# Two PSUM banks that hold K over each change of layer, and an earlier place for the filling unit's denominators and heads, in a two-layer decode kernel

## The chip, the cores and the metric

The kernel runs on one core of a Trainium2 chip. The metric is the device time of one execution in microseconds (us). Before the change the median of three runs is 2507.16 us (2505.84 to 2508.34). The profile comes from one more execution, which took 2507.28 us; its instructions span 2505.5 us.

## What is computed

Two identical rounds are run over a state `x` of 2 batches x 512 values. A round is an attention block over a cache (32 query heads in 8 groups, so 8 K and V heads of 128 values, 32768 cached positions), and then a mixer, a small MLP over each value of the normalised row:

```python
x = x + attention(layernorm(x), k_cache, v_cache, wq, wo)
x = x + mixer(layernorm(x), w1, b1, w2, b2)      # w2 @ gelu(w1 * ln(x) + b1) + b2, 1792 hidden
x = x + attention(layernorm(x), k_cache, v_cache, wq, wo)   # the same caches and weights again
x = x + mixer(layernorm(x), w1, b1, w2, b2)
```

Everything is fp32. K and V of both batches together are 536.9 MB, and both rounds read all of them, so most of the kernel is a stream of cache data from HBM.

## The kernel before

**Units, granules, steps.** A unit is (layer, batch, K/V head). It has 64 granules of K and 64 of V. A granule is 128 partitions x 512 fp32 (256 KB), and it takes one *cell* of the SBUF tile `mem`, which has 106 cells. A step consumes 4 granules: `k_step` (L333) is four score matmuls at L340 into a `scores` bank, `v_step` (L384) four matmuls at L393 into the bank `acc`. A granule's matmul shows as 2 rows of the profile, so a step is 8 rows. Between K and V of a unit lie the maximum (L354, L362), the transposes (L370) and the exponentials (L375).

**Order.** `Order` (L43) writes out the list of 1024 steps. While V of one unit runs, the K of the next has been read. At a change of layer the attention of one batch ends, its mixer runs, and the next layer's first K of that batch can only start when the mixer has given its query. `changes` (L67) names, for each of the two batches, three units: `x`, the last unit of layer 0 for the batch; `fill`, a unit of the other batch whose V is streamed while the mixer runs; and `y`, the first unit of layer 1, which has the same cache head as `x`. Since `x` and `y` read the same K and V, some of it is kept in `mem` and loaded once: `KEPT_K` = 10 granules of K and all 64 of V (L85 to L90). Those 74 cells are taken through the change, and what streams has to go through the other 32.

**Work around a change.** `at(p, f, ...)` hangs a function behind step `p` (L712). With `e` the last V step of `x` (the fill's V begins at `e` + 1): the head sums `out_1` and the output product `out_2` of `x`, the first mixer normalisation (`mix_1`, `mix_2`), seven pairs of gelu tiles with their `project` (L510) behind steps `e` + 3 to `e` + 10, `take_rows` (L468) which copies the bank `rows`, and `change_0` to `change_3` (L570 to L599) behind `e` + 11 to `e` + 14, which make the query of `y`. `unread` (L604) are matmuls whose result nobody reads; they keep TensorE busy. The filling unit's own `denominators` (L412) stand at its fifth V step, its `out_1` 7 steps and its `out_2` 9 steps behind its last V step, that is, among the K steps of `y` (L766, L781 to L783).

**PSUM.** Eight banks: two for `scores`, `acc`, `rows0` and `rows1` (one for each batch), `bcast` for the mixer's input, and two that the pool `misc` turns through for all small results and for the query products.

**Loads.** All loads are issued from one queue (SP, L833 for K and V, L828 for weights), in the order in which the steps need them, each with a count of granules, a first cell, and the step behind which it is issued. `plan_loads` (L117) chooses cells and step beforehand with its own estimates: it takes the largest piece and the highest cells that it thinks cost no wait (`reversed(spots)`, L164). The sizes around a change are laid down by `cut` (L92 to L99): the fill's V and the K of `y` come four granules at a time, except the first load of K of `y`, which has `-KEPT_K % STEP` = 2 granules. At run time the load waits until the instructions that used its cells are done.

**The end.** The last unit's V is loaded in pieces of 16, 16, 16, 8, 4, 2, 1 and 1 granules; `last_mixer` (L627) then does the last head sums, mixer and output.

Of the kernel before, what the change touches and what calls it, by code (L numbers as in the profile page):

```python
# [10 lines left out]
ALU = mybir.AluOpType  # L11
# [11 lines left out]
KEPT_V = 64  # L23
SIZES = (32, 24, 16, 8, 4)
# [18 lines left out]
class Order:  # L43


    def __init__(self, heads):
# [70 lines left out]
def plan_loads(order, weights, busy):  # L117
# [7 lines left out]
    from_kept = set(order.kept.values())  # L125
# [16 lines left out]
    while i < len(asked) or weights:  # L142
# [58 lines left out]
def gqa_mixer_kernel(ctx: ExitStack, tc: tile.TileContext, x, kt, v, wqo, cols, out):  # L201
# [6 lines left out]
    FT = (cols.shape[1] - 1) // 3  # L208
# [11 lines left out]
    pmisc = ctx.enter_context(tc.tile_pool(name="pmisc", bufs=2, space=bass.MemoryType.PSUM))  # L220
# [9 lines left out]
    cols_sb = const.tile([P, 3 * FT + 1], F32, name="cols_sb")  # L230
    w1c, b1c, w2c = (cols_sb[:, k * FT : (k + 1) * FT] for k in range(3))
    b2c = cols_sb[:, 3 * FT : 3 * FT + 1]
# [6 lines left out]
    sel1 = selg[:, 0:1].to_broadcast([P, P])  # L239
    qz = const.tile([P, 28 + 32 * SLOTS], F32, name="qz")  # L240
    acc = pfix.tile([P, G], F32, name="acc")
    rows = [pfix.tile([P, G], F32, name=f"rows{b}") for b in range(B)]
# [3 lines left out]
    xT = {}  # L246

    def constants():
# [9 lines left out]
        nc.vector.memset(acc, 0.0)  # L258
        for t in rows:
            nc.vector.memset(t, 0.0)  # L260

    def first_input():
# [4 lines left out]
        p = pmisc.tile([P, G], F32, name="misc")  # L267
# [6 lines left out]
        p = pmisc.tile([P, G], F32, name="misc")  # L274
# [12 lines left out]
    q_at, q_ps, q_row, turn = {}, {}, {}, [0]  # L287
# [13 lines left out]
    def wide_products(us, wq):  # L301

        q_ps[us] = pmisc.tile([P, G], F32, name="misc")
# [3 lines left out]
    def narrow_products(us, side):  # L307

        n = side.shape[1]
        pt = pmisc.tile([P, G], F32, name="misc")  # L310
# [43 lines left out]
    def max_1(u):  # L354
        mxa = work.tile([P, 1], F32, name="mxa")
        nc.vector.tensor_reduce(mxa, mx[u], axis=AX.X, op=ALU.max)  # L356
        pm = pmisc.tile([P, G], F32, name="misc")
# [4 lines left out]
    def max_2(u):  # L362
        pm = pmisc.tile([P, G], F32, name="misc")
# [3 lines left out]
        lsum[u] = work.tile([P, 2, R], F32, name="lsum")  # L367

# [43 lines left out]
    def denominators(u):  # L412
        pl = pmisc.tile([P, G], F32, name="misc")
# [12 lines left out]
    thin = rows[0]  # L426
    po_of = {}

    def out_sum(u):
        po_of[u] = pmisc.tile([P, G], F32, name="misc")  # L430
# [9 lines left out]
    def out_1(u):  # L440
# [5 lines left out]
        oT[u] = work.tile([P, R], F32, name="oT")  # L446
        nc.vector.tensor_mul(oT[u], po[:, :R], rl[u])  # L447
# [5 lines left out]
    def out_2(u):  # L453
        layer, b, h = u
        for r in range(R):
            nc.tensor.matmul(  # L456
                rows[b][32 * r : 32 * r + 1, :],
                oT[u][:, r : r + 1],
# [441 lines left out]
```

## Time and profile before

| | before |
|---|---|
| median of three runs | 2507.16 us |
| the profiled execution | 2507.28 us |
| its span, first to last instruction | 2505.5 us |
| TensorE busy | 1394.1 us |
| VectorE busy | 180.5 us |
| ScalarE busy | 185.8 us |
| read from HBM | 1064.33 MB |
| mean rate over the span | 425 GB/s |

PE stands for TensorE matmuls, PEld for its weight loads, DVE for VectorE, ACT for ScalarE, POOL for GpSimd, SP for the engine whose queue issues the loads. In a timeline row the columns are start, duration, engine, line, operation, output and inputs, and in brackets the idle time of the engine just before with what ended it. A chain or wait that ends in "DMA mem<-in_kt_dram" ended when a load of K landed.

### The profile page before, as it was taken

How to read it: one execution, taken by the hardware profiler on the slowest of the kernel's cores; microseconds unless marked ns; L12 is line 12 of the kernel's file. 1: busy time of each engine (PE TensorE's matmuls, PEld its weight loads, DVE VectorE, ACT ScalarE, POOL GpSimd, SP SyncE). 2: the span in 40 equal slices, each digit the busy share in tenths (PEclk: the TensorE clock that was granted, in tenths of full speed). 3: DMA queues.
4: the chain of work that ended last, by engine and by line, in shares of the span. 5: the costliest groups of instructions: out<-in, count | busy, mean ns of one | idle time of the engine just before them, and what ended most of it. 6: DMA issues, size and time to landing. Idle time of an engine off the chain costs nothing. (4 is left out here: it accounts for less than half of the span.)

```text
span 2505.5 us, 21221 instructions
## 1 busy us (share of the span) xinstructions
PE 1394.1 (56%) x9682; PEld 398.7 (16%) x9682; DVE 180.5 (7%) x487; ACT 185.8 (7%) x579; POOL 5.2 (0%) x18
## 2 busy tenths in 40 slices
PE   3455455554555545556676674555555545564567
PEld 1111111111111111112121121111111111111112
DVE  1000000000000000001010010000000000000012
ACT  0100000000000000001110100000000000000021
POOL 0000000000000000000000000000000000000000
PEclk8777777777777777778888887677777777777788
DMA  9999999999999999999999999999999999999996
GB/s 419 435 432 433 433 432 431 434 429 437 435 431 433 433 430 430 428 429 411 404 426 424 401 430 434 433 434 431 432 435 428 433 434 432 433 434 431 434 428 268
DMA packets 35523, 1065.70 MB, mean 425 GB/s; under 512 B 4197, under 2 KB 4201, under 8 KB 5354
## 3 DMA queue, kind: packets, MB, share of 16 engines
q1 hardware_dynamic: 35144, 1064.32, 98.9%
q8 instruction: 76, 1.25, 0.2%
q14 instruction: 13, 0.11, 0.0%
q10 hardware_dynamic: 290, 0.03, 0.0%
HBM read 1064.33 MB, written 0.00 MB: 425 GB/s over the span
## 5 line engine op out<-in xcount | busy, mean ns | idle before, releaser
L393 PE MATMUL acc<-mem,S 128*16 128x512 f32 x4080 | 595.8, 719 | 600.0 <-DMA mem<-in_v_dram 595.2
L340 PE MATMUL scores<-mem,qz 128*32 128x512 f32 x4096 | 607.0, 735 | 484.4 <-DMA mem<-in_kt_dram 484.2
L375 ACT ACTIVATE S<-S,neg 128x128 f32<-128x128 f32 x256 | 129.6, 509 | 2243.0 <-DVE S L370 1208.4
L340 PEld LDWEIGHTS scores<-mem,qz 128*32 128x32 f32 x4096 | 136.4, 129 | 885.1 <-issue 466.0
L393 PEld LDWEIGHTS acc<-mem,S 128*16 128x16 f32 x4080 | 125.0, 107 | 922.8 <-issue 830.8
L350 DVE TENSOR_REDUCE mx<-scores 128x1 f32<-128x512 f32 x64 | 44.3, 692 | 758.5 <-PE scores L340 750.7
L432 PEld LDWEIGHTS misc<-selg,row 128*128 128x128 f32 x256 | 50.5, 294 | 49.7 <-issue 40.1
L432 PE MATMUL misc<-selg,row 128*128 128x4 f32 x256 | 53.3, 331 | 3.3 <-DVE row L424 3.3
L370 DVE STREAM_TRANSPOSE S<-scores 128x512 f32<-128x512 f32 x64 | 45.5, 711 | 125.4 <-PE acc L393 125.4
L456 PE MATMUL rows<-mem,oT 128*1 128x512 f32 x248 | 51.2, 915 | 0.3 <-DVE oT L447 0.3
L375 ACT ACTIVATION_READ_ACCUMULATOR S<-S,neg 128x1 f32 x256 | 47.7, 186 | 0.0
L360 DVE TENSOR_REDUCE m<-misc 1x4 f32<-1x128 f32 x32 | 8.9, 279 | 381.2 <-PE misc L358 381.2
L424 DVE COPY row<-acc 128x512 f32<-128x512 f32 x32 | 22.1, 692 | 181.6 <-PE acc L393 181.6
L418 DVE RECIPROCAL rl<-misc 128x4 f32<-128x4 f32 x32 | 5.9, 183 | 369.9 <-PE misc L416 369.9
L447 DVE TENSOR_TENSOR oT<-misc,rl 128x4 f32<-128x4 f32 x32 | 5.2, 163 | 293.1 <-PE misc L432 292.6
L416 PEld LDWEIGHTS misc<-both,one 128*128 128x128 f32 x64 | 14.4, 281 | 50.6 <-issue 46.0
L305 PE MATMUL misc<-mem,xw 128*32 128x512 f32 x144 | 19.6, 618 | 1.9 <-DVE xw L281 1.9
L312 PEld LDWEIGHTS misc<-selg,row 128*128 128x128 f32 x128 | 17.1, 208 | 19.1 <-issue 10.3
L312 PE MATMUL misc<-selg,row 128*128 128x2 f32 (+1 forms) x128 | 18.5, 266 | 0.8 <-DVE row L297 0.8
L532 ACT ACTIVATE row<-bcast,bias,scale 128x512 f32<-128x512 f32 x21 | 16.3, 778 | 30.5 <-PE rows L516 15.4
L416 PE MATMUL misc<-both,one 128*128 128x4 f32 x64 | 17.2, 340 | 2.0 <-DVE both L415 2.0
L358 PE MATMUL misc<-ident,mxa 128*1 128x128 f32 x64 | 16.1, 344 | 2.1 <-DVE mxa L356 2.1
(119 smaller groups left out, 247.8 us busy)
## 6 DMA issues: line engine op xcount, KB each, us to landing
mem<-in_v_dram SPq DMA_DIRECT2D x13, 4096.0 KB, 26.6
mem<-in_v_dram SPq DMA_DIRECT2D x37, 1024.0 KB, 8.8
mem<-in_kt_dram SPq DMA_DIRECT2D x16, 2048.0 KB, 17.0
mem<-in_kt_dram SPq DMA_DIRECT2D x30, 1024.0 KB, 7.6
mem<-in_wqo_dram SPq DMA_DIRECT2D x28, 1024.0 KB, 36.4
mem<-in_kt_dram SPq DMA_DIRECT2D x7, 4096.0 KB, 30.9
mem<-in_v_dram SPq DMA_DIRECT2D x4, 2048.0 KB, 27.0
mem<-in_kt_dram SPq DMA_DIRECT2D x1, 6144.0 KB
```

The costliest lines, as they stand in the source:

```text
L305: nc.tensor.matmul(q_ps[us][32 * d : 32 * d + 32, :], xw[:, d, :], wq[:, d, :], start=True, stop=True)
L312: nc.tensor.matmul(pt[:, r * n : (r + 1) * n], q_row[us][:, r * DH : (r + 1) * DH], side, start=True, stop=True,)
L340: nc.tensor.matmul(sc_ps[u, half][32 * row : 32 * row + 32, :], qz[:, at : at + 32], cells(at_cell["K", u, g], 1), start=(i == 0), stop=(i ...
L350: nc.vector.tensor_reduce(mx[u][:, half : half + 1], sc_ps[u, half], axis=AX.X, op=ALU.max)
L370: nc.vector.transpose(S[half], sc_ps[u, half])
L375: nc.scalar.activation(s[:, :, h], s[:, :, h], AF.Exp, bias=neg[u][:, h : h + 1], scale=SCALE, accum_out=lsum[u][:, half, h : h + 1],)
L393: nc.tensor.matmul(acc[32 * row : 32 * row + R * QT, :], S[half][:, col : col + R * QT], vc, start=(g < NG), stop=(g >= quads - NG),)
L416: nc.tensor.matmul(pl[:, :R], ones, both, start=True, stop=True)
L424: nc.vector.tensor_copy(asb[u], acc)
L432: nc.tensor.matmul(po_of[u][:, :R], asb[u][:, t * DH : (t + 1) * DH], selg[:, t * R : (t + 1) * R], start=(t == 0), stop=(t == QT - 1 and ...
L456: nc.tensor.matmul(rows[b][32 * r : 32 * r + 1, :], oT[u][:, r : r + 1], wo_of(u)[:, r, :], start=(u == order.first_of[layer, b]), stop=(u ...
L532: nc.scalar.activation(hid[key, f], px[key], AF.Gelu_apprx_tanh, bias=shift[key][:, f : f + 1], scale=slope[key][:, f : f + 1],)
```

## The change

Each kept K now has two more granules, without two more cells. Behind the third K step of `x` the new `hold` copies its granules 10 and 11 from `mem` into two PSUM banks, `held0` and `held1`. Behind the first K step of `y`, when granules 0 and 1 of the kept K have been used, `give_back` copies the banks into those two cells (one copy on ScalarE, one on VectorE), where the third K step of `y` reads them. `y` no longer loads granules 10 and 11; its K is loaded from granule 12 on, in 13 loads of four.

The banks are found by joining others. `rows0` and `rows1` become one bank `rows`, in which each batch has a partition of every group of 32: the weights that were one column become two, one of them zero (`oz`, `w2z`), every product adds onto the bank (`start=False`), and `take_rows` clears its own batch's rows with a multiplication by `keep` behind its copy. The two `misc` banks become one tile with four quarters, of which `quarter()` gives the next; the query products go to `bcast`. `unread` becomes several matmuls of 128 columns. The granules of the last unit that went to `rows0` (`thin`) go to `held0`.

The filling unit's `denominators` go behind the second step of the second half of its V, its `out_1` one step and its `out_2` two steps behind its V, as for other units. Since `plan_loads` decides cells by its estimates, all cells behind the first change come out differently, the end's too.

The core of the diff:

```diff
+HELD = 2
...
+        self.held = {("K", x, KEPT_K + j): ("K", y, KEPT_K + j) for x, _, y in self.changes for j in range(HELD)}
+        self.back = {("K", y, j): ("K", y, KEPT_K + j) for _, _, y in self.changes for j in range(HELD)}
...
-            self.cut("K", y, KEPT_K, (-KEPT_K % STEP,) + (STEP,) * ((2 * HALF - KEPT_K) // STEP))
+            self.cut("K", y, KEPT_K + HELD, (STEP,) * ((2 * HALF - KEPT_K - HELD) // STEP))
...
-                        last_use[a + j] = step_of[k]
+                        last_use[a + j] = step_of[order.back.get(k, k)]
+                if key in order.held:
+                    landed[order.held[key]] = queue + LAND_US
...
-    rows = [pfix.tile([P, G], F32, name=f"rows{b}") for b in range(B)]
+    rows = pfix.tile([P, G], F32, name="rows")
+    held = [pfix.tile([P, G], F32, name=f"held{j}") for j in range(HELD)]
+    misc = pfix.tile([P, G], F32, name="misc")
...
+    def quarter():
+
+        turn[2] += 1
+        k = turn[2] % 4
+        return misc[:, k * P : (k + 1) * P]
...
+    def hold(x):
+
+        for j in range(HELD):
+            nc.vector.tensor_copy(held[j], cells(at_cell["K", x, KEPT_K + j], 1))
+
+    def give_back(y):
+
+        for j in range(HELD):
+            at_cell["K", y, KEPT_K + j] = at_cell["K", y, j]
+            to = cells(at_cell["K", y, j], 1)
+            if j % 2:
+                nc.vector.tensor_copy(to, held[j])
+            else:
+                nc.scalar.activation(to, held[j], AF.Copy)
...
-                rows[b][32 * r : 32 * r + 1, :],
-                oT[u][:, r : r + 1],
+                rows[32 * r : 32 * r + B, :],
+                oT[u][:, 2 * r + 1 - b : 2 * r + 3 - b],
...
-        nc.vector.tensor_copy(ysb[key], rows[key[1]])
+        nc.vector.tensor_copy(ysb[key], rows)
+        nc.vector.tensor_scalar_mul(rows, rows, keep[:, b : b + 1])
...
-        for _ in range(count):
-            nc.tensor.matmul(idle[0][:1, :n], one, S[0][:, :n] if u == order.last else ident[:, :1].to_broadcast([P, n]), start=True, stop=True)
+        for _ in range(count * n // P):
+            side = S[0][:, :P] if u == order.last else ident[:, :1].to_broadcast([P, P])
+            nc.tensor.matmul(idle[0][:1, :], one, side, start=True, stop=True)
...
-        at(v0 - 1 if u == order.last else v0 + 4 if fills else v_mid + 2, denominators, u, us=0.4)
+        at(v0 - 1 if u == order.last else v_mid + 2, denominators, u, us=0.4)
...
-            late = 0 if u == order.v_before[order.last] else 7 if fills else 1
+            late = 0 if u == order.v_before[order.last] else 1
             at(v_end + late, out_1, u, us=1.2)
-            at(v_end + (late + 2 if fills else 2 * late), out_2, u, us=2.0)
+            at(v_end + 2 * late, out_2, u, us=2.0)
...
+    for x, _, y in order.changes:
+        at(first["K", x] + KEPT_K // STEP, hold, x)
+        at(first["K", y], give_back, y)
```

What the planner gives the K of `y` at the first change, as first granule @ first cell : step behind which it is issued, counted from the first K step of `y` (0). All loads have four granules but the first of before. At the second change the cells are others, and the steps are the same but for the load of granule 28 of the changed kernel (0 for 1):

```
before  10@104:-4 (two granules)  12@100:-3  16@96:-2  20@92:-1  24@24:1  28@102:3  32@98:4
        36@94:5  40@102:7  44@90:7  48@98:8  52@102:10  56@94:10  60@98:12
after   12@102:-4  16@98:-3  20@94:-2  24@90:-1  28@24:1  32@20:2  36@102:3
        40@98:4  44@94:5  48@90:6  52@102:9  56@98:10  60@94:11
```

TensorE's instructions from the fill's last V steps into the first K of `y`, at the first change. `acc<-mem` is a V step, `scores<-mem` x4 a K step, `misc<-both` the fill's denominators, `misc<-selg,row` 128x4 its `out_1` and `rows<-mem` its `out_2`. Before:

```order
L516 MATMUL rows_85<-hid,cols_sb 1x256 x2
L393 MATMUL acc<-mem,S_88 16x512 x4
L562 MATMUL misc<-selg,row 128x1 x4
...
L393 MATMUL acc<-mem,S_88 16x512 x8
L340 MATMUL scores<-mem,qz 32x512 x28
L432 MATMUL misc<-selg,row 128x4 x4
L340 MATMUL scores<-mem,qz 32x512 x8
L456 MATMUL rows_86<-mem,oT 1x512 x4
L340 MATMUL scores<-mem,qz 32x512 x28
```

And now:

```order
L558 MATMUL rows<-hid,cols_sb 2x256 x2
L447 MATMUL misc<-both,one 128x4
L424 MATMUL acc<-mem,S_90 16x512 x4
L606 MATMUL misc<-selg,row 128x1 x4
...
L424 MATMUL acc<-mem,S_90 16x512 x8
L356 MATMUL scores<-mem,qz 32x512 x4
L463 MATMUL misc<-selg,row 128x4 x4
L356 MATMUL scores<-mem,qz 32x512 x4
L490 MATMUL rows<-mem,oz_81 2x512 x4
L356 MATMUL scores<-mem,qz 32x512 x56
```

The denominators came from an earlier V step to a place ahead of the eleventh, the head sums from behind the seventh K step to behind the first, and the output product from behind the ninth to behind the second; from there on K steps follow each other without other work.

VectorE's instructions at the same place; `row<-rows` is `take_rows` at the mixer's end, `row<-acc` the copy of the fill's heads. Before:

```order
L470 COPY row<-rows_85 128x512
L572 TENSOR_TENSOR xw<-misc,sq 128x4
...
L326 COPY qz<-misc 128x4
L424 COPY row<-acc 128x512
L447 TENSOR_TENSOR oT<-misc,rl 128x4
L350 TENSOR_REDUCE mx<-scores 128x1
```

And now:

```order
L506 COPY row<-rows 128x512
L507 TENSOR_SCALAR rows<-rows,keep 128x512
L446 TENSOR_TENSOR both<-lsum 128x4
L449 RECIPROCAL rl<-misc 128x4
L616 TENSOR_TENSOR xw<-misc,sq 128x4
...
L342 COPY qz<-misc 128x4
L455 COPY row<-acc 128x512
L479 TENSOR_TENSOR oz_81<-misc,rl 128x4
L396 COPY mem<-held_87 128x512
L366 TENSOR_REDUCE mx<-scores 128x1
```

The clearing multiplication and the denominators' two instructions now stand between the mixer's last copy and the sum that starts the query, and one copy back follows the fill's head scaling.

The loads of the last unit on SP, with what each waits for (a PE semaphore stands for the steps that used its cells). Before:

```order
L833 DMA mem<-in_v_dram 128x8192 [waits DMAHW3_49]
L833 DMA mem<-in_v_dram 128x4096 [waits DMAHW7_49,PE_49]
L833 DMA mem<-in_v_dram 128x2048
L833 DMA mem<-in_v_dram 128x1024
L833 DMA mem<-in_v_dram 128x512 [waits DMAHW5_49]
L833 DMA mem<-in_v_dram 128x512 [waits DMAHW6_49]
```

And now:

```order
L882 DMA mem<-in_v_dram 128x8192 [waits PE_49]
L882 DMA mem<-in_v_dram 128x4096 [waits DMAHW4_49,PE_49]
L882 DMA mem<-in_v_dram 128x2048 [waits DMAHW7_49,DMAHW5_49,PE_49]
L882 DMA mem<-in_v_dram 128x1024 [waits PE_49]
L882 DMA mem<-in_v_dram 128x512 [waits DMAHW1_49,PE_49]
L882 DMA mem<-in_v_dram 128x512 [waits PE_49]
```

Before, the last five pieces were issued behind the fourth V step of the last unit. Now the piece of 8 is issued behind its sixth V step, and those of 4, 2, 1 and 1 behind its ninth, tenth, eleventh and twelfth.

More of the change, by code (lines that the diff above doesn't have):

```diff
@@ L257, in constants @@
         )
-        nc.vector.memset(acc, 0.0)
-        for t in rows:
+        nc.vector.tensor_scalar(keep, selg[:, :B], -1.0, 1.0, op0=ALU.mult, op1=ALU.add)
+        for t in (acc, rows, *oz):
             nc.vector.memset(t, 0.0)
@@ L309, in narrow_products @@
         n = side.shape[1]
-        pt = pmisc.tile([P, G], F32, name="misc")
+        pt = quarter()
         for r in range(R):
@@ L424, in take_out @@
         nc.vector.tensor_copy(asb[u], acc)
-    thin = rows[0]
+    thin = held[0]
     po_of = {}
     def out_sum(u):
-        po_of[u] = pmisc.tile([P, G], F32, name="misc")
+        po_of[u] = quarter()
         for t in range(QT):
@@ L559, in columns @@
     def columns(key):
-        pt = pmisc.tile([P, G], F32, name="misc")
+        pt = quarter()
         for d in range(DT):
             nc.tensor.matmul(
-                pt[:, d : d + 1], ysb[key][:, d * P : (d + 1) * P], selg[:, 0:1], start=True, stop=True
+                pt[:, d : d + 1], ysb[key][:, d * P : (d + 1) * P], sel(key), start=True, stop=True
             )
```

83 lines of the change are left out of this document (50 added, 33 removed).

## The prediction, made before the changed kernel ran

> **What bounds the kernel now.** I read the page first: its slices and queue rows, and the two costliest groups.
>
> ```profile
> DMA  9999999999999999999999999999999999999996
> q1 hardware_dynamic: 35144, 1064.32, 98.9%
> L393 PE MATMUL acc<-mem,S 128*16 128x512 f32 x4080 | 595.8, 719 | 600.0 <-DMA mem<-in_v_dram 595.2
> L340 PE MATMUL scores<-mem,qz 128*32 128x512 f32 x4096 | 607.0, 735 | 484.4 <-DMA mem<-in_kt_dram 484.2
> ```
>
> The load queue is busy in every slice but the last, and TensorE's idle time ends when a load lands. So the time is the bytes at the rate of the queue, plus stretches where the queue is not full, plus the start and the end. The windows of 50 us say where it is not full: an undisturbed one, then the two in which the layer changes.
>
> ```profile
> 1300.00:1350.00 50.00, 25.55 (x150) 6.11 (x154) 2.14 (x6) 4.16 (x16) 0.00 (x0) 0.75 1.01 434
> 1200.00:1250.00 50.00, 35.86 (x229) 9.27 (x226) 4.73 (x17) 1.39 (x3) 0.54 (x1) 0.83 0.98 404
> 1400.00:1450.00 50.00, 33.13 (x200) 8.01 (x203) 5.78 (x20) 3.46 (x13) 0.54 (x1) 0.81 0.98 396
> ```
>
> The last column, GB/s, falls from 434 to 404 and 396. To see why, I read TensorE's weight loads there in order of time; at most steps the first row of a step starts when its load lands. L393 is the fill's V, L340 the K of `y`, L432 the fill's `out_1`.
>
> ```profile
> 1213.67 0.13 PEld L393 LDWEIGHTS acc<-mem,S 128*16 128x16 f32 x8 [2.38 <-DMA mem<-in_v_dram]
> 1214.12 0.13 PEld L340 LDWEIGHTS scores<-mem,qz 128*32 128x32 f32 x4 [0.31 <-issue]
> ...
> 1217.41 0.16 PEld L340 LDWEIGHTS scores<-mem,qz 128*32 128x32 f32 x8 [1.02 <-DMA mem<-in_kt_dram]
> 1219.85 0.16 PEld L340 LDWEIGHTS scores<-mem,qz 128*32 128x32 f32 x8 [2.29 <-DMA mem<-in_kt_dram]
> 1222.34 0.20 PEld L340 LDWEIGHTS scores<-mem,qz 128*32 128x32 f32 x8 [2.33 <-DMA mem<-in_kt_dram]
> 1224.83 0.20 PEld L340 LDWEIGHTS scores<-mem,qz 128*32 128x32 f32 x8 [2.28 <-DMA mem<-in_kt_dram]
> 1226.69 1.78 PEld L432 LDWEIGHTS misc<-selg,row 128*128 128x128 f32 x8 [1.66 <-issue]
> 1228.49 0.20 PEld L340 LDWEIGHTS scores<-mem,qz 128*32 128x32 f32 x8
> ...
> 1249.49 0.16 PEld L340 LDWEIGHTS scores<-mem,qz 128*32 128x32 f32 x8 [4.13 <-DMA mem<-in_kt_dram]
> ```
>
> Undisturbed, a load of four granules lands every 2.48 us (1219.85, 1222.34, 1224.83), which is 0.62 us for a granule. From the first such load of K, 1217.41, to the last of the unit, 1249.49, there are 12 periods: 29.8 us, and it took 32.1. So **2.3 us are lost**. At the second change, which has the same pattern:
>
> ```profile
> 1407.85 0.13 PEld L393 LDWEIGHTS acc<-mem,S 128*16 128x16 f32 x8 [2.35 <-DMA mem<-in_v_dram]
> ...
> 1411.60 0.16 PEld L340 LDWEIGHTS scores<-mem,qz 128*32 128x32 f32 x8 [1.02 <-DMA mem<-in_kt_dram]
> ...
> 1435.60 0.16 PEld L340 LDWEIGHTS scores<-mem,qz 128*32 128x32 f32 x8 [2.98 <-DMA mem<-in_kt_dram]
> ...
> 1443.07 0.20 PEld L340 LDWEIGHTS scores<-mem,qz 128*32 128x32 f32 x8 [2.29 <-DMA mem<-in_kt_dram]
> ```
>
> 1411.60 to 1443.07 is 31.5 us for the same 29.8: **1.7 us lost**. The loads themselves show the cause. These are three answers on times from issue to landing: three loads of the fill's V, then a load of K issued at 1230.5, then one issued at 1242.1, all of four granules.
>
> ```profile
> mem<-in_v_dram SPq DMA_DIRECT2D x3, 1024.0 KB, 8.8
> mem<-in_kt_dram SPq DMA_DIRECT2D x1, 1024.0 KB, 4.7
> mem<-in_kt_dram SPq DMA_DIRECT2D x1, 1024.0 KB, 7.3
> ```
>
> In the fill, a load is issued 8.8 us ahead: three others are in front of it. The load at 1230.5 found almost nothing in front, and needed 4.7 us, of which 2.5 are its transfer. So it must be issued some 2.2 us before the queue runs dry, and was not. It is granule 40 (40@102:7 in the planner's list): because the first load of K has two granules, the next ones lie across the fill's pieces, three pieces (102, 98, 94) take turns instead of four, and this load stands behind the eighth K step, which came late since `out_1` (1.78 us at 1226.69) stands right ahead of it.
>
> **The change part by part.** *Bytes.* Two granules at each of two changes are not loaded: 4 x 0.62 = **2.5 us** of the queue.
>
> *Order of the loads of K.* Now all 13 are of four granules on the cells of four, each issued behind the one step that used them (the planner's list). In before, the loads behind steps 7 and 12 found one other in front; now there are three or four at each, as in the fill. Take the tightest, granule 52, behind step 9: the load for that step is granule 36, and 40, 44 and 48 are still in front, 3 x 2.48 = 7.4 us, less one step. A step is 1.9 us at its slowest here (1224.83 to 1226.69), so 5.5 are left of the 2.2 needed. I count both losses as gone: 2.3 + 1.7 = **4.0 us**.
>
> The same by dates: from the fill's last V load, 13 x 2.48 = 32.2 us, so the last K lands at 1213.67 + 32.2 = 1245.9 instead of 1249.49, and 1407.85 + 32.2 = 1440.1 instead of 1443.07. That is 3.6 + 3.0 = **6.6 us**; I use 6.5, the sum of the two terms. What follows each K keeps its distance to it, and the queue stays full, so the gain should last to the end. Bounds: 2.5, if the losses come back elsewhere; and by the rates 50 x (1 - 404/434) + 50 x (1 - 396/434) = 7.8, the most that these windows could give, to which the bytes add 2.5: 10.3.
>
> *Head sums and output product, moved.* `out_1` and `out_2` leave the eighth and tenth K step, and delay the second, third and fourth instead. At full pace both are known from a usual place.
>
> ```profile
> 1214.86 0.69 DVE L424 COPY row<-acc 128x512 f32<-128x512 f32 x1 [3.96 <-PE acc L393]
> 1205.68 0.60 ACT L585 ACTIVATE row<-misc 128x512 f32<-128x512 f32 x1 [4.88 <-PE misc L305]
> 2457.72 1.05 PE L432 MATMUL misc<-selg,row 128*128 128x4 f32 x8 [0.81 <-DVE row L424]
> 2459.03 1.04 PE L456 MATMUL rows<-mem,oT 128*1 128x512 f32 x8 [0.26 <-DVE oT L447]
> ```
>
> The copy of `acc` ends at 1215.55, `out_1` 1.05 us later; with the second K step and `out_2` of about 1 us each, the third K step starts at about 1218.5, and the fourth at 1219.5, where its row now says 1217.41. Its load lands 1.2 us earlier than there, so it no longer waits for data. The loads behind these steps are issued some 2 us later; their lead of 8.8 us against 4.7 covers that: cost 0. If that lead were gone, it would be these 2 us at each change.
>
> *Copies.* `hold` is 4 copies in all of about 0.69 us on DVE, nearest row L424, beside K steps that wait for loads: 0. One load of V waits for them instead of for a step; the queue is tens of us deep there. `give_back` is a copy of 0.60 on ACT and one of 0.69 on DVE at each change. ACT has nothing to do, DVE has `out_1`'s scaling ahead (0.16), so both end by 1217.6, before the third K step wants them: 0, and 0.7 at each if DVE comes late. The multiplication by `keep` (no such row; between 0 and the 0.69 of the copy, and I take 0.69, an operation of the same size) runs 7 times, behind the copy that is waited for. The wider weights and the zeros add columns to weight loads only: 0.
>
> *Denominators.* They now wait, on PE, for `both`, which stands behind the copy of `rows` (0.69) and `keep`: about 1.6 us in which the fill's eleventh step stands still behind them. Its loads have the same 4.1 us of spare lead. The query's chain comes 1.2 us later at first and, waiting for loads at each step, about 0.3 at the end. It has room: the query was ready at
>
> ```profile
> 1210.74 0.16 DVE L326 COPY qz<-misc 128x4 f32<-128x4 f32 x1 [1.79 <-PE misc L312]
> ```
>
> and its first use is 1214.12, 3.2 us later. Cost 0; it would be the excess over 3.2.
>
> *One bank for four quarters.* A matmul into a quarter now waits when DVE is still reading another one: up to five DVE reads of 0.16 to 0.2 us in the query's chain, 1 us of the 3.2, so 0.
>
> The Trainium skill, in "PSUM — Partial Sum Buffer", section "PSUM bank collisions raise a hardware error", demands that two engines be kept apart per bank and quadrant of partitions, not per address, so it speaks against packing four results into a bank. The trace of before has no such bank; by the skill's rule the packing costs these waits, and by the 3.2 us of room they change nothing.
>
> *The end.* The last loads now hang on steps of the last V.
>
> ```profile
> 2467.00 7.64 PE L393 MATMUL acc<-mem,S 128*16 128x512 f32 x64
> 2474.46 2.74 PE L610 MATMUL misc<-S,one 128*1 128x512 f32 x6
> 2477.04 3.63 PE L393 MATMUL acc<-mem,S 128*16 128x512 f32 x32
> L833 SPq DMA_DIRECT2D mem<-in_v_dram x5: 327/434/530, 2471.3 to 2473.1; - x5
> DMA to landing us min/median/max: 10.5/13.0/13.7
> ```
>
> These five loads are the last pieces: that of 8 granules is issued at 2471.3 and lands 10.5 later, 2481.8; that of 4 lands a period later, 2484.3; the last is issued at 2473.1 and lands at 2486.8. Eight steps take 7.64 us, so the sixth ends at 2472.7; issued then, the piece of 8 needs 4.7 + 2.5 = 7.2 us: 2479.9, in time. The ninth step ends at 2477.04 + 0.9 = 2477.9; the piece of 4 needs 4.7: 2482.6, in time, and so are the small ones, each a step of 0.9 later. By the row with 7.3 instead of 4.7 the two would be 0.7 and 0.9 late. So 0 to 0.9; I take 0, since some 4 us of other loads are still in front of both, nearer to the fill's loads.
>
> **Sum.** 2507.28 (span 2505.5 and 1.8 around it) - 2.5 - 4.0 = 2500.8. The profiled execution is 0.1 above the median of the three, so I say **2500.8 us**.
>
> **The rivals.** *Only the bytes.* The lost periods come back: a queue that is full at one place runs dry at the next, for example at V of `y`, or at the end by 0.9. Against it: the fill holds 2.48 us a load with only four loads in turn. For it: at 1242.1 a load with a load in front still took 7.3 us, which my 4.7 doesn't explain. Then 2507.3 - 2.5 = 2504.8; half way 2502.8.
>
> *The end falls behind its own steps: slower.* If TensorE goes slowly there, every last piece is late, since each waits for a step. A slow pace exists:
>
> ```profile
> 2428.42 3.62 PE L393 MATMUL acc<-mem,S 128*16 128x512 f32 x16 [8.51 <-DMA mem<-in_v_dram]
> ```
>
> Two steps in 3.62, 1.8 each. Then the sixth step ends at 2477.9, the eighth at 2481.5, the unread matmuls (2.74 us in before) last 5.2, the twelfth ends at 2486.7 + 4 x 1.8 = 2493.9, and the last piece lands 3 us behind that, at 2497, where it was 2486.8: 10 us, net +3.7: 2511 us. It decides from about 1.3 us a step. Against it: the rows above, 0.95 and 0.9 a step.
>
> The Trainium skill, in "TensorE: Matmul & The Clock Gate", "Part 1: The HAM clock gate", has full clock return after about 3.4 us of steady work; the trace agrees (3.62 us slow, then 0.9 a step), and by it this rival would last two steps and cost nothing.
>
> **Chances.** Forecast 0.60, its own range 2498.5 to 2502.1. Only the bytes or half way 0.30, 2502.2 to 2505.5. The slower end 0.10, 2506 to 2513, of it 0.03 below the bound. A difference of 0.2% (5 us) is about what a measurement of this kernel can tell from no change: faster by more (below 2502.1) 0.60, within 0.33, slower 0.07. Range 2497.5 to 2506.5: it leaves out the slow end and the far bound of the rates.
>
> **What would show it.** The K of `y` without a gap over 2.6 us between steps, last K near 1245.9 and 1440.1; 1.05 MB less read; third K step at 1218.5 with its copies done before; the last pieces landing without a gap, and the stretch from there to the end as long as before. It is wrong if steps of K or of the last V wait for a load issued under 4.7 us before, or if `y` waits for its query.

## The result, and the profile after

The changed kernel takes 2502.43 us (median of 21 runs, 2500.28 to 2505.89) where the kernel before, run beside it, takes 2505.84 us (21 runs, 2502.94 to 2508.65). The ratio is 0.9987 with an interval of 0.9981 to 0.9993: 3.3 us faster, by 1.8 to 4.8. The forecast was 6.5 us faster, so the direction holds and the size is about half.

The profiled execution of the changed kernel took 2500.57 us (span 2498.6), 6.7 us less than the profiled one of before, close to the 6.5 of the sum. That agreement misleads: the one execution lies 1.9 below the median of its kernel, the other 1.4 above. Most of what follows is about that.

From the page: the load queue has the 1.05 MB less that four granules make, and it stays full. From the windows of 50 us over the two changes of layer (last column GB/s, where before had 404 and 396):

```profile
q1 hardware_dynamic: 34568, 1063.27, 99.1%
```

```profile
1200.00:1250.00 50.00, 36.01 (x240) 9.93 (x240) 7.37 (x24) 1.60 (x4) 0.54 (x1) 0.83 1.01 419
...
1400.00:1450.00 50.00, 34.52 (x229) 7.95 (x225) 5.00 (x13) 4.74 (x17) 0.00 (x0) 0.80 1.01 420
```

TensorE's weight loads at the first change, and the last K step at the second (start, busy time, engine, line; in brackets the idle time ahead and what ended it). L424 is the fill's V, L356 the K of `y`, L447 the denominators, L463 `out_1`, L490 `out_2`:

```profile
1201.44 0.30 PEld L447 LDWEIGHTS misc<-both,one 128*128 128x128 f32 x2 [2.12 <-DVE both L446]
...
1213.55 0.13 PEld L424 LDWEIGHTS acc<-mem,S 128*16 128x16 f32 x8 [1.64 <-DMA mem<-in_v_dram]
...
1215.49 0.97 PEld L463 LDWEIGHTS misc<-selg,row 128*128 128x128 f32 x8 [0.93 <-DVE row L455]
1216.47 0.16 PEld L356 LDWEIGHTS scores<-mem,qz 128*32 128x32 f32 x8
1216.93 0.10 PEld L490 LDWEIGHTS rows<-mem,oz 128*2 128x2 f32 x4 [0.30 <-DVE oz L479]
1217.36 0.10 PEld L490 LDWEIGHTS rows<-mem,oz 128*2 128x2 f32 x4 [0.33 <-issue]
1217.79 0.13 PEld L356 LDWEIGHTS scores<-mem,qz 128*32 128x32 f32 x4 [0.32 <-issue]
...
1243.67 0.16 PEld L356 LDWEIGHTS scores<-mem,qz 128*32 128x32 f32 x8 [2.27 <-DMA mem<-in_kt_dram]
1246.14 0.20 PEld L356 LDWEIGHTS scores<-mem,qz 128*32 128x32 f32 x8 [2.31 <-DMA mem<-in_kt_dram]
```

```profile
1436.96 0.16 PEld L356 LDWEIGHTS scores<-mem,qz 128*32 128x32 f32 x8 [2.32 <-DMA mem<-in_kt_dram]
```

The third K step starts at 1217.79 without waiting for `give_back`, and the last K is at 1246.14 (forecast 1245.9). By the second change the K ends at 1436.96, 6.1 earlier than in before's profile. So the K of `y` did what was forecast. The rest is in the dates at which loads land. Cut at six landings that both kernels have, the spans of the first and of a second profile of each kernel (the second ones are from the runs below) divide so, in us:

| stretch, between landings | before | before, second | changed | changed, second |
|---|---|---|---|---|
| start to granules 48-51 of the first fill's V | 1206.1 | 1206.5 | 1206.1 | 1206.5 |
| first change, to granules 30-31 of the K behind `y` | 63.0 | 62.5 | 60.5 | 61.1 |
| on to granules 44-47 of the second fill's V | 128.7 | 127.7 | 127.5 | 128.5 |
| second change, to the middle of K of (1,0,5) | 108.3 | 106.2 | 104.1 | 104.4 |
| on to the middle of V of (1,1,1) | 922.2 | 923.0 | 922.2 | 922.4 |
| to the last landing | 58.5 | 58.4 | 60.9 | 58.7 |
| last landing to the end of the span | 18.7 | 17.3 | 17.5 | 18.9 |
| span | 2505.5 | 2501.6 | 2498.6 | 2500.4 |

The first half of the program and the 922 us of layer 1 vary by less than 1 us. The changes and the stretch between them, the last pieces and the end vary more, each by up to 2.2 us from one execution to the next of the same kernel. The first pair of profiles differs by 6.9 us, the second by 1.2; the medians by 3.4.

The end is the plainest case. It is the chain behind the last V; here are the last head's product with wo and the sum behind it, from the timelines of TensorE, in before, before's second profile, the changed kernel and its second profile:

```profile
2488.50 1.78 PE L642 MATMUL scores<-mem,oT 128*1 128x256 f32 x16 [0.25 <-DVE oT L447]
2490.76 1.76 PE L652 MATMUL bcast<-mem,selg 128*128 128x512 f32 x2
```

```profile
2485.94 1.04 PE L642 MATMUL scores<-mem,oT 128*1 128x256 f32 x16 [0.25 <-DVE oT L447]
2487.49 1.12 PE L652 MATMUL bcast<-mem,selg 128*128 128x512 f32 x2 [0.31 <-ACT mem L651]
```

```profile
2482.71 1.04 PE L689 MATMUL scores<-mem,oz 128*1 128x256 f32 x16 [0.25 <-DVE oz L479]
2484.26 1.12 PE L699 MATMUL bcast<-mem,selg 128*128 128x512 f32 x2 [0.31 <-ACT mem L698]
```

```profile
2483.12 1.58 PE L689 MATMUL scores<-mem,oz 128*1 128x256 f32 x16 [0.25 <-DVE oz L479]
2485.19 1.96 PE L699 MATMUL bcast<-mem,selg 128*128 128x512 f32 x2
```

The same two groups take 2.2 us at full pace and 3.5 us at the slow one, in either kernel. The granted clock over these rows is 0.55 and 0.63 in before's first profile, 0.62 and 0.56 in the changed kernel's second, and 1.00 in the other two. Of the 6.9 us between the first two profiles, the end makes 1.2. The Trainium skill, in "TensorE: Matmul & The Clock Gate", section "Part 1: The HAM clock gate", says that the clock follows an activity window of about 3.4 us that runs free of the program. The rows agree, in that the same instructions meet either pace.

### The profile page after: what moved, and what is told of

It is laid out like the page before. It is cut to its first block, busy times and chain, and to the rows that moved or that the text cites. A ratio compares the mean times of both kernels' runs of the same rounds, so it can differ in the third digit from the quotient of the medians.

```text
span 2498.6 us, 21381 instructions
## 1 busy us (share of the span) xinstructions
PE 1382.1 (55%) x9754; PEld 410.0 (16%) x9754; DVE 188.5 (8%) x502; ACT 187.0 (7%) x581; POOL 5.2 (0%) x18
## 5 line engine op out<-in xcount | busy, mean ns | idle before, releaser
L424 PE MATMUL acc<-mem,S 128*16 128x512 f32 x4080 | 594.0, 715 | 592.6 <-DMA mem<-in_v_dram 587.7
L356 PE MATMUL scores<-mem,qz 128*32 128x512 f32 x4096 | 601.6, 728 | 491.4 <-DMA mem<-in_kt_dram 491.3
L356 PEld LDWEIGHTS scores<-mem,qz 128*32 128x32 f32 x4096 | 143.4, 127 | 881.6 <-issue 787.1
L424 PEld LDWEIGHTS acc<-mem,S 128*16 128x16 f32 x4080 | 126.5, 106 | 905.5 <-issue 819.6
L463 PEld LDWEIGHTS misc<-selg,row 128*128 128x128 f32 x256 | 48.9, 285 | 48.2 <-issue 36.8
L463 PE MATMUL misc<-selg,row 128*128 128x4 f32 x256 | 51.7, 325 | 3.3 <-DVE row L455 3.2
L490 PE MATMUL rows<-mem,oz 128*2 128x512 f32 x248 | 50.3, 899 | 0.3 <-DVE oz L479 0.3
L479 DVE TENSOR_TENSOR oz<-misc,rl 128x4 f32<-128x4 f32 x32 | 5.2, 162 | 272.1 <-PE misc L463 271.6
L447 PEld LDWEIGHTS misc<-both,one 128*128 128x128 f32 x64 | 13.9, 271 | 53.3 <-issue 46.2
L321 PE MATMUL bcast<-mem,xw 128*32 128x512 f32 x144 | 20.0, 618 | 1.7 <-POOL x_rs L294 1.7
L447 PE MATMUL misc<-both,one 128*128 128x4 f32 x64 | 16.7, 332 | 5.2 <-DVE both L446 5.2
## 6 DMA issues: line engine op xcount, KB each, us to landing
mem<-in_kt_dram SPq DMA_DIRECT2D x15, 2048.0 KB, 17.5
```

Of the source, the lines that this page charges most:

```text
L321: nc.tensor.matmul(q_ps[us][32 * d : 32 * d + 32, :], xw[:, d, :], wq[:, d, :], start=True, stop=True)
L356: nc.tensor.matmul(sc_ps[u, half][32 * row : 32 * row + 32, :], qz[:, at : at + 32], cells(at_cell["K", u, g], 1), start=(i == 0), stop=(i ...
L424: nc.tensor.matmul(acc[32 * row : 32 * row + R * QT, :], S[half][:, col : col + R * QT], vc, start=(g < NG), stop=(g >= quads - NG),)
L447: nc.tensor.matmul(pl[:, :R], ones, both, start=True, stop=True)
L463: nc.tensor.matmul(po_of[u][:, :R], asb[u][:, t * DH : (t + 1) * DH], selg[:, t * R : (t + 1) * R], start=(t == 0), stop=(t == QT - 1 and ...
L490: nc.tensor.matmul(rows[32 * r : 32 * r + B, :], oT[u][:, 2 * r + 1 - b : 2 * r + 3 - b], wo_of(u)[:, r, :], start=False, stop=(u == order ...
```

## The experiments

Ratios are to the kernel before, timed beside each run, with 95% intervals:

| run | what it is | median us | ratio |
|---|---|---|---|
| after_again | the changed kernel | 2501.32 | 0.9988 (0.9979 to 0.9997) |
| early_tail | changed, last loads earlier | 2501.07 | 0.9981 (0.9972 to 0.9990) |
| late_heads | changed, heads as before, planner free | 2506.06 | 1.0006 (0.9997 to 1.0015) |
| late_plan | changed, heads as before, same loads | 2500.95 | 0.9987 (0.9978 to 0.9996) |
| den_late | changed, denominators as before, same loads | 2501.53 | 0.9982 (0.9973 to 0.9991) |
| late_both | late_plan and early_tail | 2500.25 | 0.9977 (0.9968 to 0.9986) |
| kept8 | before with 8 granules kept | 2506.54 | 1.0002 (0.9993 to 1.0010) |
| early_heads | before, heads moved, planner free | 2508.74 | 1.0013 (1.0005 to 1.0022) |
| early_plan | before, heads moved, same loads | 2506.96 | 1.0011 (1.0002 to 1.0020) |
| out_early | before, only out_1 and out_2 moved, same loads | 2506.06 | 1.0002 (0.9993 to 1.0011) |

### Second profiles of both kernels

No edit.

> The kernel before without an edit, for a second profile of it. The first profile was 1.4 us slower than the median of its runs, and the prediction took its 4.0 us of lost periods as the kernel's. If they vary from one execution to the next, this profile has other losses in the two K of y, with the same dates elsewhere; if they are fixed, it has the same 2.3 and 1.7 us, and the spread comes from another place.

> The changed kernel without an edit, timed beside the two plans, and for a second profile of it. If the 8 us that its profile gained over the changes of layer are typical, the second profile has them too; if they are one execution's luck, it has 1 to 3 us less there, and the rest of its dates agree.

This execution of before took 2503.35 us. Its first and last K loads of four granules, at each change:

```profile
1217.71 0.16 PEld L340 LDWEIGHTS scores<-mem,qz 128*32 128x32 f32 x8 [1.01 <-DMA mem<-in_kt_dram]
...
1247.98 0.20 PEld L340 LDWEIGHTS scores<-mem,qz 128*32 128x32 f32 x8 [2.37 <-DMA mem<-in_kt_dram]
...
1410.43 0.16 PEld L340 LDWEIGHTS scores<-mem,qz 128*32 128x32 f32 x8 [1.03 <-DMA mem<-in_kt_dram]
...
1440.73 0.20 PEld L340 LDWEIGHTS scores<-mem,qz 128*32 128x32 f32 x8 [2.32 <-DMA mem<-in_kt_dram]
```

30.3 us each for the 29.8 of twelve periods: 0.5 us lost at each change, where the first profile had 2.3 and 1.7. So the loss that is counted by landing dates is not a fixed one of the kernel: it varies by 1.8 and 1.2 us between two executions. One gap in the queue is there in both: the load behind the eighth step, issued at 1230.5 in the first profile and at 1230.8 in this one, comes when the queue is nearly empty. GB/s in 40 slices of 1225 to 1255, first profile, then second:

```profile
GB/s 415 437 404 448 415 382 197 87 98 317 448 404 437 426 426 393 459 393 448 404 415 437 404 459 393 437 371 360 502 404 459 371 437 437 481 279 328 513 442 486
```

```profile
GB/s 382 459 415 382 415 393 262 76 76 218 415 415 448 404 415 426 437 404 459 382 404 448 415 360 492 371 426 415 459 481 393 502 415 415 393 388 289 492 470 437
```

Four slices of 0.75 us at 262, 76, 76 and 218 of some 415 lack 1.9 us of transfer, and the first profile's 197, 87, 98 and 317 lack 1.7. The landings show this one in part and other things besides: from the fill's V to the middle of the next K the two profiles differ by 0.5 us (table), though their K of `y` differ by 1.8. Dates of single landings are a poor count of what the queue loses.

The changed kernel's second profile took 2503.30 us (span 2500.4). By the table it is 1.9 us slower than the first from the start of the first change to the end of the second: 0.6 and 0.3 at the changes, 1.0 between them. So the first profile's gain over this part, about 8 us against before's first, was in part one execution's luck.

This second profile loses time just ahead of the change. Windows of 1195 to 1215, first this one, then late_plan (a run described below; the third column from the right is the granted clock):

```profile
1195.00:1215.00 20.00, 15.63 (x116) 6.99 (x115) 3.46 (x16) 4.98 (x7) 0.54 (x1) 0.83 0.97 393
```

```profile
1195.00:1215.00 20.00, 14.96 (x140) 6.17 (x136) 3.37 (x15) 4.98 (x7) 0.54 (x1) 1.00 1.02 424
```

And the weight loads there, in the second profile:

```profile
1201.77 0.30 PEld L447 LDWEIGHTS misc<-both,one 128*128 128x128 f32 x2 [2.12 <-DVE both L446]
...
1203.07 1.43 PEld L606 LDWEIGHTS misc<-selg,row 128*128 128x128 f32 x8 [0.85 <-DVE rl L449]
```

TensorE stands 2.12 us at the denominators, as in the first profile (1201.44), but here the clock drops right after it (L606 takes 1.43 instead of 0.97; the granted clock is 0.83 over the window, 1.00 in the first profile). The fill's V steps fall behind their loads, the loads behind those steps are issued only 5.2 to 6.2 us ahead instead of some 8, and the queue thins out: 20 x (1 - 393/424) = 1.5 us. By landing dates, the way from granules 48-51 of the fill's V to the last K of `y` is 1.3 us longer than in the first profile (41.3 for 40.0).

### The heads, with the planner free

late_heads, on the changed kernel:

```diff
-        at(v0 - 1 if u == order.last else v_mid + 2, denominators, u, us=0.4)
+        fills = [y for y, (_, fill) in changed.items() if fill == u]
+        at(v0 - 1 if u == order.last else v0 + 4 if fills else v_mid + 2, denominators, u, us=0.4)
...
-            late = 0 if u == order.v_before[order.last] else 1
+            late = 0 if u == order.v_before[order.last] else 7 if fills else 1
...
-            at(v_end + 2 * late, out_2, u, us=2.0)
+            at(v_end + (late + 2 if fills else 2 * late), out_2, u, us=2.0)
```

> The changed kernel, with the fill's denominators, out_1 and out_2 back at the places of before (behind the fill's fifth V step, the eighth and the tenth K step). Theory (the lost periods came from three pieces of four taking turns at an offset of two granules; now four take turns): the K of y keeps its pace of 2.48 us a load, time within 0.5 us of the changed kernel. Rival (the heads were the cause, since the load behind the eighth step waited for out_1): the gaps at the eighth and tenth step come back, about 2 us at each change, 4 us slower than the changed kernel and no faster than before.

early_heads is the same edit the other way round, on before.

> The kernel before, with only the move of the fill's denominators, out_1 and out_2; the planner then also puts the last five loads behind the same steps as in the changed kernel. Theory (offset of two granules, not the heads): most of the lost periods of K stay, each change gains at most 1 us, and the end costs 1.5 us: within 1.5 us of before. Rival (the heads): 4 us of lost periods go, 1.5 us come at the end: 2.5 us faster than before.

late_heads came out as the rival had it and early_heads slower than either, but not for the rival's reason. In late_heads the K of `y` at the first change keeps its gain: the last one lands at 1246.4. It loses at the second fill's V. Windows of 1350 to 1400, the changed kernel and late_heads:

```profile
1350.00:1400.00 50.00, 37.21 (x310) 13.66 (x314) 8.69 (x30) 17.99 (x35) 1.08 (x2) 0.93 1.01 419
```

```profile
1350.00:1400.00 50.00, 38.75 (x288) 12.32 (x281) 7.34 (x20) 17.37 (x34) 0.54 (x1) 0.84 0.97 377
```

The planner reckons with the costs of the heads. With them elsewhere it put the second fill's V on three pieces in turn (80, 76, 84) in both of these kernels, where the changed kernel and before have four. In late_heads its loads are issued 5.9 to 7.4 us ahead, but for one of 8.9, and the queue thins. So these two runs measure another plan of loads, not the heads.

### The heads, with the loads held fixed

The planner's costs stay where the unedited kernel has them; late_plan on the changed kernel, early_plan the same the other way round on before:

```diff
+    def planned(p, q, f, u, us):
+        at(p, f, u)
+        busy[q] = busy.get(q, 0.0) + us
...
-        at(v0 - 1 if u == order.last else v_mid + 2, denominators, u, us=0.4)
+        fills = [y for y, (_, fill) in changed.items() if fill == u]
+        d = v0 - 1 if u == order.last else v_mid + 2
+        planned(v0 + 4 if fills else d, d, denominators, u, 0.4)
...
-            at(v_end + late, out_1, u, us=1.2)
-            at(v_end + 2 * late, out_2, u, us=2.0)
+            planned(v_end + (7 if fills else late), v_end + late, out_1, u, 1.2)
+            planned(v_end + (9 if fills else 2 * late), v_end + 2 * late, out_2, u, 2.0)
```

> The changed kernel with the heads of the fill at the places of before, as in the run with late heads, but with every load on the cells and behind the step that the changed kernel has (there, the planner had moved the loads of the second change to three pieces of four in turn). Theory now (with four aligned pieces in turn the place of the heads costs nothing; what was lost with late heads came from the planner's new cells): the time of the changed kernel, within 0.7 us. Rival (late heads themselves hold the loads up): 2 to 4 us slower than the changed kernel, with periods over 2.6 us in the K of y.

> The kernel before with the heads of the fill moved to the places of the change, but with every load on the cells and behind the step of before, the last five of them too. Rival that the first runs brought up (the heads alone opened the gaps of K, either cure is enough): the loads behind the eighth and tenth step come about 2 us earlier, and it is 2 to 4 us faster than before. Theory of the prediction (offset of two granules): the loads behind steps 7 and 12 stay late, at most 1 us faster than before.

late_plan has the time of the changed kernel (2500.95 beside 2501.32): with these loads, no gain of the heads' place can be seen. early_plan is slower than before by 0.5 to 5 us, which neither theory expected. The load behind the fill's twelfth V step is issued 2.3 us later than in before, 0.7 of which its whole trace is late, and both changes take longer (64.2 and 109.5 us in the stretches above, where before has 62.5 to 63.0 and 106.2 to 108.3). This profile has a slow clock there as well (0.91 over 1195 to 1215). In den_late (next), which has that clock too but no wait at the denominators, the same load is issued 1.5 us later than in late_plan. So the profile doesn't tell the move from the clock, and why early_plan is slower stays open.

den_late moves back the denominators alone, on the changed kernel; out_early moves `out_1` and `out_2` alone, on before.

> The changed kernel and its loads, with the fill's denominators alone back behind its fifth V step; out_1 and out_2 stay behind the first and second K step. Theory (the wait of TensorE for both, 2.12 us in all three profiles with the move, delays the steps behind it, and in two of three the loads of those steps came too late): the loads behind the fill's eleventh to fifteenth V step are issued at least 8 us ahead again, and it is 0.3 to 1.3 us faster than the changed kernel. Rival (out_1 and out_2 are what the move costs, or the move costs nothing): the time of the changed kernel.

> The kernel before and its loads, with out_1 and out_2 of the fill alone moved behind the first and second K step; the denominators stay behind the fifth V step. Theory (with both moved, the 2.3 us lost came from the denominators): within 1 us of before, on either side. Rival (out_1 and out_2 early delay the loads behind the first K steps): 2 us slower than before.

den_late is not told apart from the changed kernel or from late_plan. And its profile speaks against the theory: without the 2.12 us, the loads behind the fill's twelfth to fifteenth V step are still issued only 7.1 to 7.3 us ahead, and the queue thins there, at a granted clock of 0.91.

```profile
1195.00:1215.00 20.00, 16.00 (x136) 6.79 (x132) 3.23 (x14) 4.98 (x7) 0.54 (x1) 0.91 1.01 410
```

The other profiles fit this. The clock is below 1.00 in this window in five of the thirteen; the eight at 1.00 have 418 to 424 GB/s, the changed kernel's first among them, which has the wait. kept8, with the denominators at their old place, has 0.91 and 408; early_tail (wait, 0.91) has 385, and only early_plan (wait, 0.91) keeps 421. So the thin queue goes with the slow clock and not with the wait; that the clock is the cause is likely, not shown. A thin queue need not cost much either: from granules 48-51 of the fill's V to the last K of `y` den_late takes 39.7 us, as late_plan does. How much of the second profile's 1.3 to 1.5 us the wait at the denominators adds stays open.

out_early is 0.5 us slower than before by the ratio (1.8 faster to 2.8 slower), so the 1 us that was expected fits. It shows that `out_1` in front of the eighth K step did make the gap of before at the first change: with it gone, 1225 to 1255 has no slice under 284.

```profile
GB/s 382 459 393 415 448 393 426 295 448 393 448 415 426 437 393 448 415 295 360 426 393 393 448 415 371 328 448 426 448 546 393 393 393 546 284 344 524 399 481 415
```

Its first change (61.3 us) is 1.3 to 1.8 us shorter than before's, its second (109.8) 1.5 to 3.7 longer, so nothing is left.

### The loads of K alone

kept8, on before:

```diff
-KEPT_K = 10
+KEPT_K = 8
```

> The kernel before, with eight granules of K kept over a change instead of ten, so that all loads of y's K are of four granules on the cells of four; four granules more are loaded, 2.5 us. Theory (the offset cost the periods): the K of y runs at 2.48 us a load without gaps, 4.0 to 5.6 us gained, 2.5 lost: 1.5 to 3 us faster than before. Rival (only bytes count, gaps come back elsewhere): 2.5 us slower than before.

It is 0.5 us slower by the ratio (1.8 faster to 2.5 slower), with four granules (2.5 us) more to load. That is between the two expectations and excludes neither for certain; by the ratio itself some 2 us were gained. But the K did not run without gaps, as the theory had it. First and last loads of four granules, and the widest periods:

```profile
1215.95 0.24 PEld L340 LDWEIGHTS scores<-mem,qz 128*32 128x32 f32 x8 [0.62 <-DMA mem<-in_kt_dram]
...
1244.01 0.20 PEld L340 LDWEIGHTS scores<-mem,qz 128*32 128x32 f32 x8 [2.87 <-DMA mem<-in_kt_dram]
...
1249.80 0.20 PEld L340 LDWEIGHTS scores<-mem,qz 128*32 128x32 f32 x8 [3.13 <-DMA mem<-in_kt_dram]
```

33.9 us for 13 periods, 1.6 lost. Its loads are aligned like the changed kernel's and are issued only 6.7 to 9.0 us ahead of their landing; the changed kernel's in its first profile, 7.9 to 13.7, since two of them (granules 28 and 32) go to further pieces, on cells 24 and 20. This depth is the likely reason why its K rides over late heads and a slow clock where kept8's does not; no run gave kept8 the two pieces.

### The last loads

early_tail, on the changed kernel:

```diff
+LAST = ((48, 58), (56, 66), (60, 70), (62, 72), (63, 73))
...
+        self.spots = {("V", self.last, g): (c,) for g, c in LAST}
...
-            spots = range(CELLS - s + 1)
+            spots = order.spots.get(label, range(CELLS - s + 1))
```

> The changed kernel, with the last five loads of the last V put into cells that come free after its second to fourth step instead of its sixth to twelfth. Theory (the time is the queue's gaps: the change gained about 8 us over the two changes of layer in its profile, and its last loads gave back some 1.5 because the piece of eight granules was issued only 3.6 us before the one ahead of it landed): that piece lands 4.9 us behind the piece of sixteen instead of 6.3, the others follow at full pace, and the kernel is 1.3 to 1.7 us faster than the changed one. Rival (the gap at the end has another cause than the time of issue): the 6.3 us stay and the time is that of the changed kernel.

The piece of eight lands 4.91 us behind that of sixteen. The issue of the five last loads and their times to landing, in the changed kernel's first profile and in early_tail:

```profile
L882 SPq DMA_DIRECT2D mem<-in_v_dram x5: 327/328/328, 2465.9 to 2473.7; - x5
...
DMA to landing us min/median/max: 7.4/7.6/9.9
```

```profile
L884 SPq DMA_DIRECT2D mem<-in_v_dram x5: 327/374/428, 2463.0 to 2465.5; - x5
...
DMA to landing us min/median/max: 12.5/14.4/14.9
```

From the landing of the piece of sixteen to the last landing, the seven profiles in which the five loads were issued early (before's two, kept8, out_early, early_plan, early_tail, late_both) have 9.91 to 9.95 us. The six with the late places have 11.61, 10.17 (the changed kernel's two), 10.33, 10.74, 10.51 and 10.18 (late_plan, den_late, late_heads, early_heads): 0.2 to 1.7 us more, 0.7 on the mean. So the gap comes from the time of issue, as the theory had it; its 1.5 us was the worst of the six. In time, early_tail is 1.5 us below the changed kernel by the ratios (0.9981 and 0.9987), as forecast, but the intervals overlap.

late_both is late_plan with this edit.

> The changed kernel with both things that the runs found to cost: all heads of the fill at their places of before with the loads of the changed kernel, and the last five loads on cells that come free earlier. Theory: 0.8 to 1.4 us faster than the changed kernel, 4 to 5 us faster than before (ratio 0.9980 to 0.9985). Rival (each of the two was scatter): the time of the changed kernel, ratio 0.9987.

It is the fastest, 0.9977: 5.8 us below before by the ratio (3.5 to 8.0), a little more than the 4 to 5 expected, where the changed kernel in its two series has 0.9987 and 0.9988. The intervals overlap, so its lead over the changed kernel is likely, not settled.

## Why the forecast was right in direction and too large

**Bytes, 2.5 us.** The queue moved 1.05 MB less, and the K loads keep 2.48 us each. Nothing speaks against the term; no run took it alone.

**Order of the loads, 4.0 us.** This is the term that was mis-sized. The mechanism was right: at the first change the gap behind the eighth step is gone in all six profiles with the changed kernel's loads (no slice of 1225 to 1255 under 317). The amount was read from one execution, as twelve periods against landing dates, and the second profile gives 1.0 where the first gave 4.0. By the stretches of the table, in the mean of two profiles of each kernel, the two changes are 2.0 and 3.0 us shorter, of which 1.24 each are bytes: 2.5 us for the order in place of 4.0. The four other profiles with these loads have 59.4 to 60.3 and 103.9 to 104.7 in the two stretches; with them it would be 3.0. The three runs ahead of the prediction, 2.5 us apart, were a warning that a term of 4.0 read from one of them is not firm.

**The reason for the gap.** The prediction put the gap down to the offset of two granules with `out_1` ahead of the step. At the first change either cure closes it: out_early moves `out_1`, kept8 removes the offset (no slice of 1225 to 1255 under 295), and late_plan has the changed loads with `out_1` at its old place (none under 344). But closing this gap was not enough: out_early lost as much at the second change, and kept8 1.6 us at other steps of its K. What the changed kernel has beyond both is depth: two loads on further pieces, where out_early has one and kept8 none. That this is what keeps the gain is likely, not shown.

**Heads moved, cost 0; and denominators, cost 0.** With the same loads their place makes no difference that these runs can tell (late_plan and after_again), so 0 was right for the changed kernel, but not for the reason given. The prediction gave the denominators 1.6 us and 4.1 us of spare lead. The wait is 2.12 us (the multiplication by `keep` took 0.75 of it, where 0.69 was taken), and in the second profile, with a slow clock right after it, the lead is used up and 1.5 us of transfer are lost. On before's loads, which have less depth, the kernel with the move is slower (1.0011, 1.0002 to 1.0020).

**Copies, one bank in quarters.** 0, as said: the two copies end at 1216.1 and 1217.4, and the third K step at 1217.79 does not wait for them; late_plan, which has the single bank and the copies, is as fast as the changed kernel. No run took the single bank alone.

**The end, 0 to 0.9, taken as 0.** It cost 0.2 to 1.7, on the mean 0.7. The slower rival's steps of 1.8 us did not come. What came was the smaller thing, on the mean within its bounds and at worst beyond them: in the first profile the piece of eight granules, issued 3.6 us before the piece ahead of it landed, took 9.9 us from issue to landing where the prediction reckoned 7.2; in the second, issued as early, it took 8.7. One reading behind that rival was wrong too: the slow stretch at 2428.42 lasts 5.6 us and not 3.62, since the next 16 rows are slow as well and the granted clock is 0.50 until 2434.0. It covers about four steps, not two.

**The sum.** 2.5 for bytes and 2.5 for the order, less 0.7 at the end, make 4.3; the medians say 3.4 and their interval 1.8 to 4.8. The gain lies between the bytes alone (2.5) and the case that the prediction called half way (4.5). That the absolute time, 2500.8, is only 1.6 below the median of 2502.43 is in part luck: the sum started from an execution 1.4 above the median of before and took off 3.1 too much.

## What to carry to other kernels

A loss that is read from one profile may be that execution's alone: lay it beside the spread of the times, and where it is as large as the spread, price it at a range from nothing up to it. When a change moves work that a planner reckons with, hold the plan fixed in one run and let it go in another, since the effect can be the plan's, as in late_heads. In a kernel bound by its loads, count how far ahead each load is issued; look first at the ones with the least lead, and the ones at the very end count too.

## What the runs showed of the hardware that was not expected

The same load of 1 MB (granule 40) needed 4.7 and 4.5 us from issue to landing in the two profiles of before, and 7.2 us in early_plan. There, by the pace of the loads ahead (an estimate from their landings), some 2.9 us of transfer were still in front of it, and it landed 4.3 us behind them instead of 2.5. So the lead that a load needs is not one number in these runs. In before's second profile the queue moved 76 GB/s for 1.5 us while that load started.

TensorE's slow clock strikes the same instructions in one execution and not in the next. At the end of the program that is worth 1.4 us of the 3.9 by which before's two profiles differ. Ahead of the first change about as much went, through late loads, in the one profile where the clock was lowest there (0.83), though nearly all of the 2500 us are set by the loads. How much of the 6 us by which the times of one kernel spread it makes was not measured.
